# Text shift by transposing sums and one fold, text V shifted while leaving PSUM, one pass per P tile, text gate moved to the output phase: a tuned joint-attention block on one Trainium2 core

## The chip, the cores and the metric

The kernel runs on one core of one Trainium2 chip. The metric is device microseconds from start to end of one execution; lower is better. A run also lists its **span**, which is what the profiler covers of it. For the kernel before, the time is about 1.8 us more than the span.

A ratio below is the mean time of one kernel's runs over the mean of the other's runs of the same rounds, so it is not quite the ratio of the medians quoted beside it.

## The reference

Two streams, image (2 x 256 tokens) and text (2 x 32 tokens), width D = 1152, all bf16. Each is normalised, scaled and shifted by rows computed from `c`, projected to Q, K and V, and attended jointly; the outputs are gated.

```python
mod_i = (_silu(c) @ wmod_img).reshape(B, 6, 1, D)      # shift, scale, gate are the first three
mod_t = (_silu(c) @ wmod_txt).reshape(B, 6, 1, D)
hi = _layernorm(x_img, axis=-1) * (1 + sci) + shi
ht = _layernorm(x_txt, axis=-1) * (1 + sct) + sht
qkvi = hi @ wqkv_img
qkvt = ht @ wqkv_txt
# q, k, v: text tokens and image tokens concatenated, text first
scores = jnp.einsum('bqd,bkd->bqk', q, k) * D ** (-0.5)
p = _softmax(scores, axis=-1)
a = jnp.einsum('bqk,bkd->bqd', p, v)
out_i = x_img + gai * (ai @ wo_img)
out_t = x_txt + gat * (at @ wo_txt)
```

## The kernel before

The order of the work is: normalise the image rows; image V (tiles `vps`) and the image's shift rows; image Q and K (nine blocks each, one 128-column block at a time, tiles `ps`), with the text's small work hung between blocks; text Q and K; scores (`sps`) and softmax; text V; transposes of P (`pT_ps`); attention (`aps`); output products with gate and residual.

Image V is computed without its shift, and the shift's contribution (the row `sv` = shift times the V weights) is added to the attention output instead, because the rows of P sum to one. The text's V must then have the same image row subtracted, so that the addition is right for text keys too. Here, four extra matmuls do that inside the text V products, with a selector `sel` of minus ones:

```python
def v_txt(r):
    ps = ps_mm.tile([P, KT, LW], f32, tag="mm")
    for kt in range(KT):
        for g in range(2):
            mm(ps[64 * g:64 * g + NTT], lhsT=hT_t[:, kt, :], rhs=group(w_v_t, kt, 2 * r + g),
               start=(kt == 0), stop=False, tile_position=(0, 64 * g))
    for g in range(2):
        mm(ps[64 * g:64 * g + NTT], lhsT=sel[:, 2 * r + g, :], rhs=svr[:],
           start=False, stop=True, tile_position=(0, 64 * g))
    return ps

def v_txt_out(r, ps):                      # four VectorE copies, and later one more of the whole tile
    for g in range(2):
        dst = v_t[0:NTT, :].rearrange("p (c g l) -> p g c l", g=NGG, l=LW)[:, 2 * r + g]
        pin(nc.vector.tensor_copy(dst, ps[64 * g:64 * g + NTT]))
```

The text's shift row is `silu(c) @ W`. VectorE multiplies and adds the weights' nine row blocks into `acc_sh` (128 partitions x 1152 for each batch row). The sum over partitions is then made by TensorE: the float32 sums are split into two bf16 halves, and 16 matmuls with a one-column selector `pick` add the partitions:

```python
def vec_split(acc):
    ...
    for b in range(B):
        nc.scalar.copy(hl[:, 0, b, :], acc[:, b, :])
        pin(nc.vector.tensor_sub(hl[:, 1, b, :], acc[:, b, :], hl[:, 0, b, :]))

def vec_rows(hl, gps, strip):
    terms = [(b, t) for b in range(B) for t in range(2)]
    for b, t in terms:
        for g in range(NGG):
            mm(gps[LW * g:LW * g + LW], lhsT=pick[:, b, :], rhs=strip(hl[:, t, b, :], g), ...)
```

P (the softmax result) is written by VectorE in pieces: the 256 image keys, and then the 32 text keys twice, because the attention reads them from two partition ranges. Then P is transposed, copied by ScalarE, and used:

```python
def soft_div(key, parts):
    ...
    pin(nc.vector.tensor_scalar_mul(pb[0:qn, 0:NI], e[0:qn, 0:NI], rs[0:qn, :]))
    for r0, r1, b in parts:
        pin(nc.vector.tensor_scalar_mul(
            pb[r0:r1, NI:PBW].rearrange("p (h b n) -> p b h n", h=2, b=B)[:, b],
            e[r0:r1, NI:NTOK].unsqueeze(1).to_broadcast([r1 - r0, 2, NT]), rs[r0:r1, :]))
```

Each gate row is a product of 36 matmuls; it goes to DRAM and comes back spread over the partitions (`gb` for the image, `gbf` for the text). The DMAs of this trip are issued by POOL:

```python
def mod_rows(w_blk, si):
    ...                                    # 36 matmuls into gps, ScalarE copies them to g_sb
    for b in range(B):
        nc.gpsimd.dma_start(gsc[si, b, :].rearrange("(g j) -> g j", g=NGG), g_sb[b:P:32, :])

def img_gate():
    mod_rows(w_ga_i, 0)
    for b in range(B):
        nc.gpsimd.dma_start(gb[:, b, :], gsc[0, b, :].partition_broadcast(P))
```

The order in this stretch, and the order of the last weight loads on the sync queue:

```python
w_q_t, w_k_t, w_ga_i, w_v_t = ...          # loads, issued early in the program
w_ga_t = load_w(2, wmod_txt, 2 * D)        # text gate weights
w_o_i = load_rows(3, wo_img, 0)            # image output weights, in three parts
w_o_t = load_rows(1, wo_txt, 0)
...
scores and softmax, with img_gate() between   # [cut]
vt = [v_txt(r) for r in range(2)]
v_txt_out(0, vt[0])
p_transposes(0)
p_transposes(1)
v_txt_out(1, vt[1])
pin(nc.vector.tensor_copy(v_t[64:64 + NTT, :], v_t[0:NTT, :]))
txt_gate()
for d0 in range(0, KT, 3):
    attn_pair(...)
out_img(0, C3); out_img(1, C3); out_img(2, C3); out_txt(); out_img(3, ...)
```

## Time and profile before

| | before |
|---|---|
| time, median of the first 3 runs | 118.73 us (118.64 to 118.84) |
| span of the profiled run | 117.0 us, granted clock 0.995 |
| TensorE busy | 111.2 us, 95% |
| VectorE busy | 74.6 us, 64% |
| ScalarE busy | 44.4 us, 38% |
| DMA rate from 12 us to 96 us | about 410 GB/s |

The first section of the page of the kernel before gives busy time, share of the span and count of instructions for each engine; the slices below it give the DMA rate in 40 equal parts of the span.

```profile
...
PE 111.2 (95%) x1046; PEld 63.9 (55%) x1054; DVE 74.6 (64%) x158; ACT 44.4 (38%) x91; POOL 11.1 (10%) x34
...
GB/s 98 368 374 390 409 407 409 411 410 414 411 399 372 410 410 413 404 411 413 413 410 413 414 402 414 414 401 414 408 406 411 406 401 376 177 100 6 101 50 101
...
```

TensorE (PE) is busy nearly all the time, and DMA is full up to slice 33. Busy shares are averages, so they only suggest the bound. The chain of waits shows it: it follows the work that ended last back to its causes, in order of time. Its columns are start, length, and what ran; "issue" is time in which nothing was waited for. These are the pieces of the kernel before that the change touches.

```profile
...
64.32 1.71 PE gps L61 x52
66.02 0.16 issue
...
76.68 2.92 PE sps L61 x36
...
83.02 2.57 PE ps L61 x40
85.59 1.11 PE pT_ps L64 x18
86.70 1.22 PE gps L61 x36
87.92 5.88 PE aps L61 x54
93.81 19.52 PE ps L61 x144
...
113.34 0.44 DVE tmp L690
...
```

From the first of these lines to 113.32 us everything on the chain is TensorE, end to end but for pieces marked "issue" of 0.16 us (66.02) and 0.05 us. The 0.16 us stands where the record of one matmul is missing (17 of 18 are in the trace for the two blocks that follow), so it may be no pause at all. The line of 52 matmuls at 64.32 holds 36 for the text's scale row and the 16 selector matmuls of its shift; the line of 40 at 83.02 holds 36 matmuls of text V and the four selector matmuls; the 36 at 86.70 are the text gate.

What comes off this list comes off the time, as long as no hole opens. VectorE waits on PE in this part, not the other way round. In this trace the text gate weights landed at 85.71 us, 0.9 us before their first use at 86.64, and the last third of the image output weights at 92.98 us, under 2 us before its use.

The cost of the text gate's trip comes from the view of one tile, here `gbf` of the kernel before:

```profile
...
DMA to landing us min/median/max: 3.8/4.8/5.2
```

### The profile page before, as it was taken

The page shows a single profiled execution, that of the slowest core. Times are in us where ns is not written, and L with a number is a line of the kernel's source. Part 1 is how long each engine was busy: PE and PEld are TensorE (multiplying, and loading weights), DVE is VectorE, ACT ScalarE, POOL GpSimd, SP SyncE. Part 2 cuts the span into 40 slices and gives each one's busy share as a digit, 9 for nine tenths or more (in the row PEclk, how much of TensorE's full clock was granted, in tenths as well). Part 3 has the DMA queues.
Part 4 walks back from the last instruction along what each step waited for, and adds up shares of the span by engine and source line. Part 5 has one row for each costly group of instructions (what it writes and reads, how often), then busy time and mean ns, then how long its engine had stood idle before and what let it go on. Part 6 is the DMA issues. An engine that isn't in the chain of part 4 may idle for free.

```text
span 117.0 us, 2513 instructions
## 1 busy us (share of the span) xinstructions
PE 111.2 (95%) x1046; PEld 63.9 (55%) x1054; DVE 74.6 (64%) x158; ACT 44.4 (38%) x91; POOL 11.1 (10%) x34
## 2 busy tenths in 40 slices
PE   4998899999999999999999999999999999999990
PEld 1245544445574444445444658777876666656660
DVE  2368694053867979999996350018984756666671
ACT  4599720042654834325265224245556610000000
POOL 7230000000000000000000000001318018000000
PEclk9999999999999999999999999999999999999998
DMA  3999999999999999999999999999999999520223
GB/s 98 368 374 390 409 407 409 411 410 414 411 399 372 410 410 413 404 411 413 413 410 413 414 402 414 414 401 414 408 406 411 406 401 376 177 100 6 101 50 101
DMA packets 18613, 40.86 MB, mean 349 GB/s; under 512 B 1019, under 2 KB 1547, under 8 KB 18603
## 3 DMA queue, kind: packets, MB, share of 16 engines
q1 hardware_dynamic: 17728, 39.56, 87.0%
q0 software_dynamic: 480, 0.89, 2.1%
q10 hardware_dynamic: 395, 0.26, 0.7%
q8 instruction: 8, 0.13, 0.4%
q14 instruction: 2, 0.02, 0.0%
HBM read 39.38 MB, written 1.34 MB: 348 GB/s over the span
## 4 chain that ended last, share of the span: by engine, by line
PE 85%; ACT 5%; DMA 4%; DVE 2%; issue 1%; DVEq 0%
PE ps L61 53%; PE vps L61 15%; PE gps L61 6%; PE aps L61 5%; PE sps L61 4%; DMA x_i<-in_x_img_dram 4%; ACT xn_i L202 2%; ACT xn_i L201 2%; PE pT_ps L64 1%; DVE xn_i L216 1%; PE tp L64 1%; DVE tmp L690 1%; ACT rstd L211 1%; ACT rstd L212 1%; DVE o L691 0%
## 5 line engine op out<-in xcount | busy, mean ns | idle before, releaser
L61 PE MATMUL ps<-xT_i,t 128*128 128x512 bf16 x157 | 35.2, 380 | 0.4 <-issue 0.2
L61 PEld LDWEIGHTS <-t 128*128 128x128 bf16 x324 | 20.5, 98 | 19.1 <-issue 0.5
L427 DVE SCALAR_TENSOR_TENSOR acc_sh<-t,sTf,acc_sh 128x1152 f32<-128x1152 bf16 x16 | 21.4, 1414 | 0.0
L61 PE MATMUL ps<-t,aT 128*128 128x384 bf16 (+3 forms) x153 | 20.2, 308 | 0.0
L61 PE MATMUL vps<-t,hS_i 128*128 128x512 bf16 (+1 forms) x106 | 17.8, 325 | 0.2
L61 PEld LDWEIGHTS <-aT 128*128 128x128 bf16 (+1 forms) x153 | 13.0, 101 | 7.1 <-issue 0.5
L61 PEld LDWEIGHTS <-hS_i 128*128 128x128 bf16 x108 | 9.0, 98 | 8.8 <-DVE hS_i L268 0.5
L690 DVE TENSOR_TENSOR tmp<-ps,gb 128x384 bf16<-128x384 f32 (+2 forms) x13 | 6.8, 526 | 6.3 <-PE ps L61 6.3
L370 ACT CAST qkT<-ps 128x512 bf16<-128x512 f32 (+2 forms) x11 | 6.0, 552 | 11.0 <-PE ps L61 11.0
L61 PE MATMUL wps<-warm 128*128 128x512 bf16 x24 | 8.1, 498 | 1.7 <-DVE unit L132 1.5
L515 POOL DMA_DIRECT2D mod_scratch<-g_sb x4 | 2.5, 633 | 74.6 <-ACT g_sb L513 74.5
L368 ACT ACTIVATE qkT<-ps 128x512 bf16<-128x512 f32 (+2 forms) x11 | 6.1, 559 | 9.1 <-PE ps L61 9.1
L184 DVE CAST v_i<-vps 128x512 bf16<-128x512 f32 x5 | 3.5, 692 | 7.5 <-PE vps L61 7.5
L554 DVE TENSOR_REDUCE nmx<-sps 128x1 f32<-128x288 f32 x4 | 1.8, 458 | 9.9 <-PE sps L61 9.9
L186 ACT CAST v_i<-vps 128x512 bf16<-128x512 f32 x4 | 2.3, 578 | 10.0 <-PE vps L61 10.0
L623 DVE TENSOR_SCALAR aT<-aps,svc 128x288 bf16<-128x288 f32 x9 | 4.3, 518 | 2.5 <-PE aps L61 2.5
L61 PEld LDWEIGHTS <-warm 128*128 128x128 bf16 x25 | 2.7, 118 | 5.5 <-issue 2.9
L61 PEld LDWEIGHTS <-sT 128*32 128x32 bf16 x180 | 4.6, 96 | 2.0 <-issue 1.3
L61 PE MATMUL sps<-qkT 128*128 128x288 bf16 (+1 forms) x54 | 5.5, 287 | 0.0
L61 PE MATMUL gps<-t,sT 128*32 128x288 bf16 x144 | 5.2, 287 | 0.0
L61 PE MATMUL aps<-pT,v_i 128*128 128x288 bf16 x36 | 5.1, 288 | 0.0
L61 PE MATMUL ps<-hT_t,t 128*128 128x64 bf16 x162 | 5.1, 193 | 0.0
(114 smaller groups left out, 109.2 us busy)
## 6 DMA issues: line engine op xcount, KB each, us to landing
t<-in_wqkv_txt_dram SPq DMA_DIRECT2D x3, 2592.0 KB, 17.8
t<-in_wmod_img_dram SPq DMA_DIRECT2D x2, 2592.0 KB, 13.0
t<-in_wqkv_img_dram SPq DMA_DIRECT2D x2, 2592.0 KB, 20.1
t<-in_wmod_txt_dram SPq DMA_DIRECT2D x2, 2592.0 KB, 15.9
t<-in_wmod_txt_dram SPq DMA_DIRECT2D x3, 864.0 KB, 14.7
t<-in_wo_img_dram SPq DMA_DIRECT2D x3, 864.0 KB, 12.8
t<-in_wo_txt_dram SPq DMA_DIRECT2D x3, 864.0 KB, 12.6
t<-in_wqkv_img_dram SPq DMA_DIRECT2D x3, 576.0 KB, 9.1
```

The source lines that it names most:

```text
L61: return pin(nc.tensor.matmul(*a, **k))
L64: return pin(nc.tensor.transpose(*a, **k))
L184: nc.vector.tensor_copy(out_ap, in_ap)
L186: nc.scalar.copy(out_ap, in_ap)
L201: pin(nc.scalar.activation(junk, x_ap, ACT.Copy, scale=1.0 / D, accum_out=sm[:, 0:1]))
L202: pin(nc.scalar.activation(junk, x_ap, ACT.Square, scale=float(D) ** -0.5, accum_out=sm[:, 1:2]))
L368: nc.scalar.mul(out_ap, in_ap, SCALE)
L370: nc.scalar.copy(out_ap, in_ap)
L427: pin(eng.scalar_tensor_tensor(acc[:, b, :], w[:, kt, :], sTf[:, kt, b:b + 1], acc[:, b, :], op0=ALU.mult, op1=ALU.add))
L515: nc.gpsimd.dma_start(gsc[si, b, :].rearrange("(g j) -> g j", g=NGG), g_sb[b:P:32, :])
L623: nc.vector.tensor_scalar(dst, tiles[(b, dt)][:], bias, None, op0=ALU.add)
L690: nc.vector.tensor_mul(tmp[:, 0:n], ps[:, 0:n], gb[:, b, c0:c0 + n])
```

## The change

The intent is to take 20 selector matmuls out of TensorE's stream, and to arrange the rest so that TensorE still waits for nothing.

1. **Text shift.** VectorE sums the accumulated products in blocks of 32 with a transposing reduce, which leaves 36 columns in place of 1152 for each batch row, 72 in all; two matmuls with a folding matrix and two small VectorE instructions finish it.
2. **Text V.** The image row `sv` is written to DRAM and spread over the text rows by DMA (`svb`), and VectorE subtracts it while the product leaves PSUM. The loads from the text's K weights on are issued after this spread.
3. **P tiles.** VectorE writes 288 columns in one pass; POOL writes the second copy of the 32 text columns. The transposes of P come right after the scores, and the second group's PSUM copy is split over two tiles. The loads of the image gate are issued by POOL behind these writes (`img_gate_spread`).
4. **Text gate.** Its matmuls and its DRAM trip move from before the attention to the middle of the output products. The image output weights are therefore loaded before the text gate's weights.
5. The text's normalisation moves from VectorE to ScalarE, and some loads are cut differently.

```diff
+    w_o_i = load_rows(4, wo_img, 0)                 # now first ...
+    w_ga_t = load_w(3, wmod_txt, 2 * D)             # ... and the text gate's weights after it
...
+        for b in range(B):
+            nc.scalar.dma_start(svd[b].rearrange("(c g l) -> g c l", g=NGG, l=LW), svr[b:P:LW])
+        for g in range(2):
+            for b in range(B):
+                r0 = 64 * g + NT * b
+                nc.sync.dma_start(svb[r0:r0 + NT, :], svd[b, g * HD:(g + 1) * HD].partition_broadcast(NT))
...
-    def vec_split(acc): ...
-    def vec_rows(hl, gps, strip): ...
+    def shift_blocks():
+        for b in range(B):
+            pin(nc.vector.tensor_reduce(uf[:, b, :], acc_sh[:, b, :].rearrange("p (c l) -> p c l", l=LW),
+                                        axis=AX.X, op=ALU.add, apply_transpose=True))
+        pin(nc.vector.tensor_copy(ub[:, 0], uf[:]))
+        pin(nc.vector.tensor_sub(ub[:, 1], uf[:], ub[:, 0]))
+    def shift_fold():
+        ps = ps_tr.tile([P, B * KT, NGG], f32, tag="tr", name="shps")
+        for h in range(2):
+            mm(ps[:].rearrange("p k a -> p (k a)"), lhsT=fold[:].rearrange("p g l -> p (g l)"),
+               rhs=ub[:, h].rearrange("p b c -> p (b c)"), start=(h == 0), stop=(h == 1))
+        ...                                          # mask with band, sum 4 columns each
...
-        for g in range(2):
-            mm(ps[64 * g:64 * g + NTT], lhsT=sel[:, 2 * r + g, :], rhs=svr[:], ...)
...
+        pin(nc.vector.tensor_sub(v_t[:, r * VC:(r + 1) * VC], ps[:], svb[:, r * VC:(r + 1) * VC]))
...
-        pin(nc.vector.tensor_scalar_mul(pb[0:qn, 0:NI], e[0:qn, 0:NI], rs[0:qn, :]))
-        for r0, r1, b in parts: ...
+        pin(nc.vector.tensor_scalar_mul(pb[0:qn, 0:NTOK], e[0:qn, :], rs[0:qn, :]))
+        pin(nc.gpsimd.tensor_scalar(pb[0:qn, NI + 2 * NT:NI + 3 * NT], e[0:qn, NI:NTOK], rs[0:qn, :], 0.0,
+                                     op0=ALU.mult, op1=ALU.add))
...
-    vt = [v_txt(r) for r in range(2)]
-    v_txt_out(0, vt[0])
     p_transposes(0)
+    for r in range(2):
+        v_txt_out(r, v_txt(r))
     p_transposes(1)
-    txt_gate()
+    img_gate_spread()
...
-    out_img(1, C3)
+    out_img(1, C3, between=txt_gate)
```

## The prediction

> **What bounds it now.** TensorE. The profile page's first section has PE busy 95% of a 117.0 us span at a granted clock of 0.995. In the chain of waits PE is 85%; from 12.5 us to 113.3 us it is nearly unbroken matmul. PE's list of waits holds 1.5 us before warm-up and 0.6 us of crumbs. VectorE (64%) and ScalarE (38%) bind nowhere in between. DMA is full (about 410 GB/s) until 97 us, but PE never waits for a weight. Only what leaves PE's stream, or opens a hole in it, can move the time.
>
> **What leaves PE** (chain of waits, in order of time):
> - Sixteen selector matmuls of the text shift. 52 matmuls took 1.71 us at 64.3 us; the same 36 alone took 1.22 us elsewhere: 0.49 us. Two folding matmuls of 72 columns replace them, estimated 0.1 us.
> - Four matmuls that subtract the image's shift row from text V: 40 matmuls took 2.57 us, 36 by their spacing 2.31 us: 0.26 us.
> - The 36 text gate matmuls (1.22 us) move to the output phase; not saved.
>
> Sum: about -0.65 us, all on the chain.
>
> **Off the chain.** VectorE loses two subtractions of 1.36 us, the text normalisation (0.86), eight small P writes (0.24 each), four V evictions (0.45) and a copy (0.45); it gains two transposing sums (estimated 1.3 us each) and small ones. ScalarE: -2.3 us of copies, +1.3 us of normalising. POOL: five writes of 32 columns.
>
> **Where a hole could open.**
> 1. Fold, at block 7 of K. VectorE's sums done by 63 us, fold near 67 us; the text activations then need about 1.3 us while PE has 1.97 us of block 7. No wait.
> 2. First P transposes now follow the scores directly (near 82.5 us). The text P tile is written about then; POOL's part comes behind its two DMA issues. Wait 0 to 0.3 us. v_txt then covers the second group's softmax and the PSUM copies.
> 3. Attention starts about 1.8 us earlier (near 86.0), outputs near 92. Image gate rows landed near 95 before; VectorE will wait for them at the first output chunk, but six PSUM buffers absorb it.
> 4. The text gate makes its DRAM round trip during output: store issued near 100 us, landing near 103.7, loads to about 109, against text output's first PSUM at 107.6. This trace shows 3.8 to 5.2 us to landing per hop. The Trainium skill ("DMA: Bandwidth & Descriptors", Anatomy of one DMA) gives about 2.0 us fixed; the trace's numbers are used. VectorE may stand 1.5 us, then recovers 0.5 us per chunk before the last; most of it vanishes.
>
> **Prediction: 118.1 us**, range 117.4 to 118.9. Chance of over 2% faster 0.04, within 2% 0.92, over 2% slower 0.04.
>
> **What would show it right.** Outputs start about 1.8 us earlier, and the gain shrinks to 0.6 us once the gate matmuls run there; PE's idle time unchanged; selector groups gone; VectorE's busy time down some 6 us without effect on the end; a VectorE wait at the first gate product and perhaps at the text output.
>
> **What would make it wrong.** Text gate landing after 111 us: VectorE ends last, slower by 1 us or more. PE waiting on POOL at the P transposes or on VectorE before text Q. Smaller DMAs on the sync queue delaying weights. A larger gain would need idle time in the head to shrink; its chain (input DMA, ScalarE sums, normalisation) is untouched.

## The result, and the profile after

| | before | after |
|---|---|---|
| median of 6 runs | 118.78 us (118.54 to 118.88) | 118.15 us (118.08 to 118.50) |
| ratio | | 0.9954, 95% interval 0.9938 to 0.9969 |
| span of the profiled run | 117.0 us, clock 0.995 | 116.3 us, clock 1.0 |

The time is 118.15 us where 118.1 was predicted. The verdict at 2% is "same"; the gain of half a per cent is outside the noise of these runs. A second series, on another chip, did not show it by time (after_again below).

The first section of the page of the kernel after:

```profile
...
PE 110.3 (95%) x1036; PEld 63.3 (54%) x1036; DVE 71.9 (62%) x151; ACT 44.8 (38%) x93; POOL 12.3 (11%) x34
...
```

TensorE's busy time is 0.9 us lower, VectorE's 2.7 us. The chain of waits of the kernel after, over the same stretch:

```profile
...
60.26 1.22 PE gps L61 x36
...
67.41 0.07 PE shps L61 x2
...
76.29 2.93 PE sps L61 x36
...
82.63 0.50 PE pT_ps L64 x9
83.13 2.33 PE ps L61 x36
85.46 0.61 PE pT_ps L64 x9
86.07 5.78 PE aps L61 x54
91.84 5.85 PE ps L61 x36
97.69 1.22 PE gps L61 x36
98.91 13.77 PE ps L61 x108
...
112.71 0.43 DVE tmp L693
...
```

The scale row is 36 matmuls alone (1.22 us), the shift two matmuls in 0.07 us, and text V 36 matmuls in 2.33 us. The text gate (1.22 us at 97.69) now stands between two pieces of the output products. TensorE is again unbroken.

The two chains can be cut at the same points and compared. Each number is the difference of two starts in the chains above and their earlier lines (first image V matmul at 14.53 us before and 14.37 after).

| stage | before, us | after, us | difference |
|---|---|---|---|
| start to first image V matmul | 14.53 | 14.37 | -0.16 |
| first image V matmul to scores | 62.15 | 61.92 | -0.23 |
| scores to attention | 11.24 | 9.78 | -1.46 |
| attention | 5.89 | 5.77 | -0.12 |
| outputs, to VectorE's last four instructions | 19.53 | 20.87 | +1.34 |
| VectorE's last four instructions | 1.22 | 1.21 | -0.01 |

The -1.46 is the gate's 1.22 leaving and 0.24 of text V; the +1.34 is the gate's 1.22 coming back and 0.12 more. The sum from the first image V matmul on is -0.48 us. I use this stretch, **from the first image V matmul to the end of VectorE's last output instruction**, as the yardstick for single profiles below: 100.03 us before, 99.55 us after. It leaves out the head, whose end depends on when the image scale weights land, and which none of the five parts was meant to touch. The clock is no rival to it: the windows view gives a granted clock of 1.00 from 15 us to 113 us in all kernels but onepass_only; the 0.995 of the kernel before comes from the time after its last matmul.

Two of VectorE's groups after (line, engine, operation, output<-input, count | busy us, mean ns | idle before, releaser) show the transposing sums and one large idle time:

```profile
...
L445 DVE TRANSPOSE_TENSOR_REDUCE uf<-acc_sh 128x36 f32<-128x1152 f32 x2 | 2.6, 1346 | 0.0
...
L455 DVE TENSOR_TENSOR uf<-shps,band 128x72 f32<-128x72 f32 x1 | 0.2, 233 | 4.4 <-PE shps L61 4.4
...
```

The transposing sums took 1.35 us each, as estimated. The 4.4 us in front of `uf<-shps` is VectorE waiting for TensorE to reach the fold, so the fold had that much slack.

Two more numbers were different from what was predicted. The text gate's trip back, by the view of the tile `gbf` of the kernel after:

```profile
...
DMA to landing us min/median/max: 2.0/2.2/2.5
```

And the DMA rate while the spread of the V shift was under way, by the view of windows (busy time and count of each engine, clock, DMA share, GB/s), first of the kernel before and then of the kernel after:

```profile
...
58.00:62.00 4.00, 4.00 (x21) 1.76 (x19) 4.00 (x4) 2.54 (x3) 0.00 (x0) 1.00 1.05 414
...
```

```profile
...
58.00:62.00 4.00, 4.00 (x50) 2.00 (x49) 3.86 (x6) 1.17 (x2) 0.00 (x0) 1.00 1.06 353
...
```

The DMA engines were as busy as before but moved 353 GB/s in place of 414. What this costs is the subject of several experiments.

### The profile page after: what moved, and what is told of

It is laid out like the page before. It is cut to its first block, busy times and chain, and to the rows that moved or that the text cites. A ratio compares the mean times of both kernels' runs of the same rounds, so it can differ in the third digit from the quotient of the medians.

```text
span 116.3 us, 2500 instructions
## 1 busy us (share of the span) xinstructions
PE 110.3 (95%) x1036; PEld 63.3 (54%) x1036; DVE 71.9 (62%) x151; ACT 44.8 (38%) x93; POOL 12.3 (11%) x34
## 3 DMA queue, kind: packets, MB, share of 16 engines
HBM read 39.52 MB, written 1.34 MB: 351 GB/s over the span
## 4 chain that ended last, share of the span: by engine, by line
PE 86%; DMA 8%; DVE 1%; SPq 1%; issue 0%; DVEq 0%
PE ps L61 53%; PE vps L61 15%; DMA t<-in_wmod_img_dram 8%; PE gps L61 5%; PE aps L61 5%; PE sps L61 5%; PE pT_ps L64 1%; PE sc_ps L61 1%; SPq L104 1%; PE tp L64 1%; DVE tmp L693 1%; DVE o L694 0%; SPq L108 0%; PE tpt L64 0%; DVE hS_i L264 0%
## 5 line engine op out<-in xcount | busy, mean ns | idle before, releaser
L61 PE MATMUL ps<-xT_i,t 128*128 128x512 bf16 x162 | 35.7, 379 | 0.0
L580 POOL TENSOR_SCALAR pb<-e,rs 128x32 bf16<-128x32 f32 (+1 forms) x5 | 2.1, 415 | 74.7 <-DVE rs L577 74.6
L61 PE MATMUL wps<-warm 128*128 128x512 bf16 x25 | 7.4, 452 | 1.5 <-DVE unit L127 1.5
```

Of the source, the lines that this page charges most:

```text
L61: return pin(nc.tensor.matmul(*a, **k))
L580: pin(nc.gpsimd.tensor_scalar(pb[0:qn, NI + 2 * NT:NI + 3 * NT], e[0:qn, NI:NTOK], rs[0:qn, :], 0.0, op0=ALU.mult, op1=ALU.add))
```

## The experiments

**Theory A**: the gain is what left TensorE's stream, 0.49 us for the fold and 0.26 us for text V less about 0.1 for the folding matmuls; everything else is neutral. **Rival B**: VectorE's lighter load is what gains (softmax, P tiles and evictions come sooner, and TensorE meets fewer late inputs). After the first four runs a third one was formed, called **E**: the V spread by DMA costs about one microsecond by delaying all later weights, and the new order of weights with the late text gate is what makes that free. The remaining parts are then not gains of their own but conditions for the others.

For reference, the yardstick of every profile, and the mean of what each kernel's timed runs took beyond their spans. Ratios are against the kernel before on the same chip.

| kernel | median, us | ratio, 95% interval | yardstick, us | time less span, us |
|---|---|---|---|---|
| before (three chips) | 118.60 to 118.81 | | 100.03 | 1.79 to 1.82 |
| after | 118.15 | 0.9954 (0.9938 to 0.9969) | 99.55 | 2.03 |
| fold_only | 118.35 | 0.9968 (0.9947 to 0.9990) | 99.60 | 1.80 |
| vshift_only | 119.83 | 1.0085 (1.0060 to 1.0110) | 100.71 | 2.04 |
| onepass_only | 124.50 | 1.0488 (1.0462 to 1.0514) | 105.59 | 1.79 |
| gate_late_only | 119.51 | 1.0080 (1.0048 to 1.0112) | 100.65 | 1.83 |
| gate_back | 120.47 | 1.0166 (1.0143 to 1.0189) | 101.13 | 2.09 |
| pe_back | 118.99 | 1.0028 (1.0008 to 1.0049) | 100.09 | 2.05 |
| dve_back | 118.35 | 0.9980 (0.9951 to 1.0009) | 99.44 | 2.06 |
| spread_only | 119.73 | 1.0088 (1.0067 to 1.0108) | 100.64 | 2.03 |
| after_again | 119.04 | 1.0008 (0.9961 to 1.0055) | 99.58 | 2.10 |
| dve_back_again | 118.70 | 0.9997 (0.9958 to 1.0036) | 99.41 | 2.09 |
| onepass_pinned | 118.58 | 0.9998 (0.9958 to 1.0037) | 100.01 | 1.82 |
| gate_later | 119.46 | 1.0066 (1.0025 to 1.0108) | 100.37 | 1.96 |

The first four kernels do one part alone on the kernel before. All kernels gave correct results.

### fold_only: the text shift's sums and fold alone

```diff
-    def vec_split(acc): ...          # and vec_rows, txt_rows_shift, txt_cols_shift
+    def shift_blocks(): ...          # as after
+    def shift_fold(): ...
-    qk_img(w_k_i, 1, {1: (txt_transposes, txt_shift_split,),
-                      6: (txt_rows_scale, txt_rows_shift, txt_cols_shift, txt_modulate),
+    qk_img(w_k_i, 1, {1: (txt_transposes, shift_blocks,),
+                      6: (txt_rows_scale, shift_fold, txt_modulate),
```

> The kernel before with the folded text shift alone: transposing sums and one pair of 72-column matmuls in place of the sixteen selector matmuls, everything else as before. Theory A (what leaves TensorE's stream is the gain): 0.49 us leave, about 0.07 to 0.1 us come, so -0.40 us, ratio to before about 0.9966, and the chain's TensorE piece at the folded place 0.4 us shorter. Rival B (relief of VectorE and ScalarE is the gain): VectorE loses only 2.7 us of subtractions and gains 2.6 us of sums here, so about 0. Rival C (a shorter head or a better order of DMAs is the gain): 0.

Measured: 118.35 us against 118.71, ratio 0.9968; the yardstick is 0.43 us shorter. The chain of waits of this kernel:

```profile
...
64.29 1.22 PE gps L61 x36
...
65.67 10.55 PE ps L61 x189
...
```

Scale row and fold now take 1.38 us from 64.29 to 65.67, where the kernel before took 1.86 (64.32 to 66.18, with the 0.16 us at the missing record in it). The safer number is the stretch from the first image V matmul to the first score matmul in the traces: 61.56 us against 61.99, or 0.43 us less. Theory A holds for this part, and the fold is the only part that gains by itself.

### vshift_only: the V shift at the eviction alone

```diff
-            mm(ps[64 * g:64 * g + NTT], lhsT=sel[:, 2 * r + g, :], rhs=svr[:], ...)
+            nc.sync.dma_start(svb[r0:r0 + NT, :], svd[b, g * HD:(g + 1) * HD].partition_broadcast(NT))
+        pin(nc.vector.tensor_sub(v_t[:, r * VC:(r + 1) * VC], ps[:], svb[:, r * VC:(r + 1) * VC]))
     # the loads from w_k_t on follow the spread on the sync queue, as after; their own order is before's
```

> The kernel before with text V's shift taken off while leaving PSUM (rows spread by DMA, four matmuls gone), the V text tile in two halves, and the six last weight loads issued after the shift rows in program order. Theory A: four matmuls, two at a time, are 0.24 to 0.26 us of TensorE's stream, so -0.25 us, ratio about 0.998. Rival B: VectorE loses 1.2 us between scores and attention, but TensorE waits for none of it, so under A nothing further; if relief there matters it would show as more than -0.4 us. Rival C: 0.

Measured: 119.83 us, ratio 1.0085. This was a miss: a gain was expected and there is a loss of a microsecond. TensorE's waits in this kernel (longest first: engine, tile, line, what it waited for, us in total, times, longest):

```profile
...
PE gps L61 <- DMA t<-in_wmod_txt_dram: 0.6, 1, 0.6
```

Its chain of waits goes through a weight load for the first time:

```profile
...
79.91 15.25 DMA t<-in_wo_img_dram
...
95.21 18.70 PE ps L61 x138
...
```

The text gate's weights landed at 86.91 us (85.71 before), the last third of the image output weights at 95.17 (92.98 before). The yardstick closes, by the starts of TensorE's instructions: from the first text V matmul to the gate +0.41 (-0.24 for the four matmuls, +0.65 at the gate's weights, of which the list of waits shows 0.59), and +0.26 in the outputs, where the seventh matmul starts at 95.21 us, 0.43 us after the sixth in place of 0.16; together with under 0.02 elsewhere that is the measured +0.68. So DMA was a second bound just under the first. My reading "PE never waits for a weight" was true and misleading.

### spread_only: the DMA spread alone, with nobody using it

This was run later, to separate the spread from the eviction.

```diff
     # kernel before, selector matmuls and all
+        for b in range(B):
+            nc.scalar.dma_start(svd[b].rearrange("(c g l) -> g c l", g=NGG, l=LW), svr[b:P:LW])
+        for g in range(2):
+            for b in range(B):
+                nc.sync.dma_start(svb[r0:r0 + NT, :], svd[b, g * HD:(g + 1) * HD].partition_broadcast(NT))
     # the loads from w_k_t on follow it on the sync queue
```

> The kernel before plus the spread of the shift rows by DMA into a tile that nobody reads, with the six last weight loads issued after it in program order; all matmuls and VectorE work as before. Theory E (DMA was the second bound, with under 1 us to spare at the text gate and under 2 us at the output weights): later weights land 1.0 to 1.2 us later, TensorE waits for the text gate weights or for the last rows of the image output weights, +1.0 to +1.5 us, ratio 1.008 to 1.013. If the loss of the run with the V shift alone came from its new V tile, row order or VectorE work instead: 0, ratio 1.000.

Measured: 119.73 us, ratio 1.0088, the same loss as vshift_only within the noise (yardstick 100.64 against 100.71). Its chain of waits holds the same weight load, 15.25 us long and ending at 95.44. The window of the spread:

```profile
...
58.00:62.00 4.00, 4.00 (x19) 1.79 (x19) 4.00 (x4) 1.75 (x3) 0.00 (x0) 1.00 1.06 352
...
```

So the spread alone makes the loss of vshift_only; the four matmuls that leave there gain nothing, because the last weights land no sooner. The four DMAs carry 147 KB, and the window lost 62 GB/s for 4 us, or 248 KB. Together, at 411 GB/s, that is an estimate of 0.96 us of DMA time. The landings agree: text Q's weights landed at 61.07 us against 59.78 and text K's at 67.79 against 66.22, but the text's scale weights, ahead of the spread, were already 0.60 us later in this profile (53.98 against 53.38). From the scale weights to text K's it took 13.81 us against 12.84, or 0.97 us more (vshift_only 13.85, the kernel after 13.82). The packets in the traces show where it went: those of the spread took 0.44 us of the 16 engines' time, and the weights' packets of 2,304 bytes took 108 to 111 ns each from 58 to 62 us in place of 93. The Trainium skill, in "DMA: Bandwidth & Descriptors", section "Issuing engines are not separate DMA queues", says that DMAs started by different engines run on the same 16 DMA engines and interleave. The interleaving shows here: text Q's weights were issued at 38.5 us, before the spread, and landed late all the same. Both were issued by the sync engine, though, so this run doesn't test engines against each other; the traces of the text gate do (POOL's loads, 3.8 to 5.2 us with the sync engine's weights under way and 2.0 to 2.5 us without), and they are in line with the page.

### onepass_only: the P tiles in one VectorE pass and POOL's copy alone

```diff
-        pin(nc.vector.tensor_scalar_mul(pb[0:qn, 0:NI], e[0:qn, 0:NI], rs[0:qn, :]))
-        for r0, r1, b in parts: ...
+        pin(nc.vector.tensor_scalar_mul(pb[0:qn, 0:NTOK], e[0:qn, :], rs[0:qn, :]))
+        pin(nc.gpsimd.tensor_scalar(pb[0:qn, NI + 2 * NT:NI + 3 * NT], e[0:qn, NI:NTOK], rs[0:qn, :], 0.0,
+                                     op0=ALU.mult, op1=ALU.add))
```

> The kernel before with one VectorE pass per P tile and the repeated 32 columns written by POOL, nothing else. Theory A: no matmul leaves, and before's TensorE did not wait for the P tiles, so 0 within 0.1 us (ratio 0.999 to 1.001). Rival B: VectorE is lighter by some 1.2 us just before the P transposes, so a gain of some 0.2 us or more.

Measured: 124.50 us, ratio 1.0488, a loss of 5.8 us. This was the largest miss. TensorE's waits:

```profile
...
PE pT_ps L64 <- POOL pb L569: 2.8, 1, 2.8
...
PE pT_ps L64 <- DVE pb L568: 0.9, 1, 0.9
```

The order of POOL's instructions in this kernel (start, length, instruction, idle time before it and its releaser):

```profile
...
81.61 1.51 POOL L515 DMA_DIRECT2D mod_scratch<-g_sb  x2 [0.70 <-ACT g_sb L513]
87.57 1.13 POOL L524 DMA_DIRECT2D gb<-mod_scratch  x2 [4.46 <-DMA mod_scratch<-g_sb]
88.74 0.56 POOL L569 TENSOR_SCALAR pb<-e,rs 64x32 bf16<-64x32 f32 x2
...
```

POOL issues the image gate's store, then stands 4.46 us until that store has landed because its next instruction is the issue of the load, and only then writes text P. The short P writes take 0.3 to 0.5 us; the wait in front of them is what costs. TensorE's two waits are 3.7 us of the 5.56 us that the yardstick lost. The rest is in the chain right behind them:

```profile
...
90.32 0.93 PE pT_ps L64 x7
91.25 2.28 PE gps L61 x28
93.53 5.99 PE aps L61 x54
...
```

The text gate's 36 matmuls (the chain counts 28 of them) took 2.35 us here by the view of the timeline, against 1.29 us in the kernel before. From 90.3 us to 93.7 us the granted clock was 0.50. Half of these 3.4 us, an estimate of 1.7 us, closes the sum to within 0.2 us. All five timed runs of this kernel show a mean clock of 0.969 to 0.986. The lower clock came right after the pause and is absent in onepass_pinned, where the pause is gone; what sets it was not tested.

The Trainium skill, in "PSUM — Partial Sum Buffer", section "Engine vs sequencer instructions", says that the queues of ScalarE, VectorE and GpSimdE are strict FIFO; this timeline agrees, and shows that the issue of a DMA that must wait holds the computing instructions behind it as well.

### onepass_pinned: the same, with the gate's load behind POOL's writes

This was run later, to confirm the reading.

```diff
     # onepass_only
-            nc.gpsimd.dma_start(gb[:, b, :], gsc[0, b, :].partition_broadcast(P))      # in img_gate()
+            pin(nc.gpsimd.dma_start(gb[:, b, :], gsc[0, b, :].partition_broadcast(P))) # after the P transposes' code
```

> The kernel before with one VectorE pass per P tile and POOL's repeat, and the image gate's loads pinned behind POOL's writes, as the whole change has them. If the 5.8 us loss of the run without the pin came from POOL's queue alone (a write to P standing behind a DMA that waits for its landing), this is 0 within 0.2 us of before, ratio 0.998 to 1.002, and TensorE shows no wait for POOL. If the pass itself or the other column offset costs, a loss of 0.3 us or more stays.

Measured: 118.58 us, ratio 0.9998, yardstick 100.01 against 100.03. POOL's order is now this:

```profile
...
81.45 1.51 POOL L515 DMA_DIRECT2D mod_scratch<-g_sb  x2 [0.70 <-ACT g_sb L513]
82.99 0.30 POOL L571 TENSOR_SCALAR pb<-e,rs 64x32 bf16<-64x32 f32 x1
...
87.42 1.17 POOL L526 DMA_DIRECT2D gb<-mod_scratch  x2 [2.48 <-DMA mod_scratch<-g_sb]
...
```

Text P is written 1.5 us after the store's issue in place of 7, and the loss is gone. The one-pass write by itself is worth nothing, because it unloads VectorE where VectorE has time. That the diff moves this load behind the P writes is not tidying: on the kernel before, the one pass without it lost 5.8 us. The whole change without it was not run. VectorE did 1.0 us less work here (73.5 us busy against 74.6), just before the P transposes, and the yardstick didn't move: that speaks against rival B at this place.

### gate_late_only: the text gate in the output phase alone

```diff
-    txt_gate()
-    out_img(1, C3)
+    out_img(1, C3, between=txt_gate)
     # and the residual's text rows are loaded with the image gate, as after
```

> The kernel before with the 36 text gate matmuls moved into the output phase, after the fourth output chunk, and the order of V and P transposes left as before. Theory A with covers: the matmuls are only moved, but before's order used their 1.2 us to cover ScalarE's two copies of the transposed P (0.88 us each) and VectorE's copies of text V. Without them attention waits, so +0.3 to +0.6 us, and TensorE's waits show the copies. Rival D (the gate's new place is itself a gain): -0.2 us or better. Plain count of matmuls without covers: 0.

Measured: 119.51 us, ratio 1.0080; the direction was right and the loss larger (0.62 us by the yardstick, 0.5 us of it a wait). The chain of waits:

```profile
...
85.69 0.62 PE pT_ps L64 x9
...
86.34 0.89 ACT pT L611
...
87.27 5.94 PE aps L61 x54
...
```

With the gate's matmuls gone from before the attention, TensorE reaches the attention while ScalarE is still copying the transposed P (0.89 us at 86.34), and TensorE waits 0.5 us. In the kernel before, the gate was cover for that copy. In the kernel after, other work is: the P transposes of the first group come before text V (2.33 us), so their copy is done in its shadow, and the second group's copy is split. That order needs P early, which is why the one-pass write belongs to the change; this last link is read from the order of the code and was not tested by itself.

### gate_back: the kernel after with the text gate back before the attention

```diff
-    w_o_i = load_rows(4, wo_img, 0)
-    w_ga_t = load_w(3, wmod_txt, 2 * D)
+    w_ga_t = load_w(2, wmod_txt, 2 * D)
+    w_o_i = load_rows(4, wo_img, 0)
+    txt_gate()                                  # before the attention
-    out_img(1, C3, between=txt_gate)
+    out_img(1, C3)
```

> The kernel after with the text gate put back in front of attention and its weights loaded ahead of the image output weights again (the load order of before); the V spread by DMA stays. If the gate's new place is worth nothing by itself (the prediction's view: only moved), the time stays at that of after, ratio to before 0.9954. If the new place is what pays for the spread's DMA time (theory E, from the run with the V shift alone, where every later weight landed 1.0 to 1.2 us late), the text gate weights land near 87 us, TensorE needs them near 86.1, waits about 0.8 us, and the image output weights' last rows come just in time or late: +0.8 to +1.3 us on after, ratio to before 1.002 to 1.006.

Measured: 120.47 us, ratio 1.0166, more than expected. TensorE's waits:

```profile
...
PE gps L61 <- DMA t<-in_wmod_txt_dram: 1.4, 1, 1.4
...
```

The gate's weights landed at 86.96 us, and TensorE was ready for them 1.44 us earlier: later weights and an earlier consumer. The yardstick is 1.58 us above the kernel after, 101.13 against 99.55. So the late gate together with the output weights ahead of it in the queue is what pays for the spread; the two were only undone together. In the kernel after, the gate's weights landed only at 95.78 us, and they were needed at 97.69.

### pe_back: the kernel after with TensorE's removed work put back

```diff
-        rows["sc"] = mod_rows_of(w_sc_t, sT32)
+        rows["sc"] = mod_rows_of(w_sc_t, sT32, extra=4)        # 16 more matmuls, results overwritten
+        for g in range(2):                                     # in v_txt: 2 more matmuls for each half
+            mm(ps[64 * g:64 * g + NTT, :], lhsT=hT_t[:, 0, :], rhs=w_v_t[:, 0, g * HD:g * HD + VC],
+               start=True, stop=True, tile_position=(0, 64 * g))
```

> The kernel after with as many idle matmuls as the change took away: sixteen 32-column-tile matmuls of 288 columns ahead of the text scale rows and four 64-column-tile ones in front of text V, into the same PSUM before the real start, so the result stays right. Theory A (the gain is TensorE's stream): the 0.49 + 0.25 us come back, so after + 0.7 us, ratio to before 1.000 to 1.002. Rival B (VectorE's and ScalarE's relief is the gain): stays at that of after, 0.9954.

Measured: 118.99 us, ratio 1.0028, yardstick 100.09. The chain of waits shows the two groups at their old lengths:

```profile
...
60.43 1.71 PE gps L61 x52
...
83.59 2.57 PE ps L61 x40
...
```

VectorE keeps its lighter load here, and the whole gain is gone. This speaks for theory A and against B. Everything else of the change is kept too, the text's normalisation on ScalarE and the new cuts and order of the loads (part 5 and rival C, neither run by itself): together with the two folding matmuls it nets 0.06 us on the yardstick (100.09 against 100.03), so no gain is left for it to explain.

### dve_back and dve_back_again: the kernel after with VectorE work put back

```diff
         pin(nc.vector.tensor_sub(ub[:, 1], uf[:], ub[:, 0]))
+        for n in range(3):                                     # 4.1 us of VectorE, nobody reads it
+            dead = work.tile([P, D], bf, tag="dead", bufs=1, name="dead")
+            pin(nc.vector.tensor_sub(dead[:], acc_sh[:, n % B, :], x_i[:, n, :]))
```

> The kernel after with three dead VectorE subtractions of 1152 elements (about 1.36 us each, 4.1 us) right behind the two sums, in front of the text scale. VectorE then has put back more than the change took from it there. Theory A: VectorE waited 4.4 us for the fold in after, so the sums still end before TensorE comes to the fold; no change against after, ratio to before 0.9954 within 0.001. Rival B: a good part of the gain is lost, ratio 0.998 or more.

Measured in the first run: 118.35 us, ratio 0.9980 with an interval from 0.9951 to 1.0009. That interval holds both theories' numbers, so the times decided nothing. The trace did: the 4.14 us were done at 65.7 us, VectorE still waited 0.55 us for the fold's matmuls, and the yardstick was 99.44 us. VectorE's timeline:

```profile
...
61.52 4.14 DVE L451 TENSOR_TENSOR dead<-acc_sh,x_i 128x1152 bf16<-128x1152 f32 x3
...
67.66 0.23 DVE L458 TENSOR_TENSOR uf<-shps,band 128x72 f32<-128x72 f32 x1 [0.55 <-PE shps L61]
...
```

The same kernel was run again beside the kernel after on one chip, with this expectation:

> The kernel after with the three dead VectorE subtractions, run once more beside the control, because the first time its interval held both answers. Theory A: the same time as the control within 0.15 us, span 116.1 to 116.4 us. Rival B: 0.25 us or more above the control, span 116.5 us or more.

Measured: 118.70 us, below its control at 119.04, yardstick 99.41 against 99.58. Putting back more VectorE time than the change took away (4.1 us against 2.7 net) cost nothing that the yardstick shows, and nothing by time within the noise. Rival B is refuted, at this place in the program.

### after_again: the control on another chip

The kernel is unchanged.

> The kernel after, unchanged, as the control on the same chip as the others of this call. Ratio to before 0.9954 within 0.0015; the span near 116.1 to 116.3 us.

Measured: 119.04 us, ratio 1.0008 with an interval from 0.9961 to 1.0055, so the gain of the first runs was not seen again by time. This is a miss. The chain of waits of its profile shows where the time was:

```profile
...
2.12 10.50 DMA t<-in_wmod_img_dram
...
15.11 13.77 PE vps L61 x63
...
```

The scale weights landed at 12.62 us where they landed at 11.85 in the first profile, and the first image V matmul began 0.74 us later. From there on it took 99.58 us against 99.55. So the yardstick of the kernel after is reproduced to 0.03 us (that of the kernel before has one profile, and onepass_pinned, with the same matmuls, has 100.01), but a head that varies by more than the gain can hide it. On this chip the kernel before varied from 118.01 to 119.46 us.

### gate_later: the text gate one output block later still

```diff
-    out_img(1, C3, between=txt_gate)
-    out_img(2, C3)
+    out_img(1, C3)
+    out_img(2, C3, between=txt_gate)
```

> The kernel after with the text gate three output chunks (4.4 us) later. By the prediction's own reasoning on the gate's two DRAM hops, with the 2.0 to 3.4 us per hop that after's trace shows in this phase: store near 104 us, loads landing near 111 us, VectorE stands from 107.6 to 111 us, does 1.5 us for the text and 3.1 us for four image chunks, and ends near 115.6 us instead of 113.9: +1.3 to +2.0 us on after, ratio to before 1.006 to 1.012. If only the count of matmuls mattered: 0.9954.

Measured: 119.46 us, ratio 1.0066; the yardstick is 100.37, or 0.82 us above the kernel after. The mechanism is as expected and the size smaller. The chain of waits ends in VectorE:

```profile
...
101.83 1.25 PE gps L61 x36
...
103.78 1.66 DMA mod_scratch<-g_sb
...
107.36 3.02 DMA gbf<-mod_scratch
...
111.67 0.56 DVE tmp L693
...
```

The store landed 1.66 us after its issue and the last load 3.02 us after its own, at 110.38 us where the expectation had about 111; VectorE then works almost without a pause from 110.5 us to the end, for 4.1 us where 4.6 were expected. The kernel after escapes this: its loads had landed by 106.98 us, 0.6 us before the text's first product at 107.6.

## Why the prediction was right, and where it was wrong

**The bound and the sum: right.** TensorE's stream bounds both kernels. Taken alone, the fold was worth 0.43 us on the yardstick (0.39 by the prediction's sum of 0.49 less 0.1), and text V 0.24 us in the stage from scores to attention (0.26 predicted). pe_back takes the gain away, dve_back and dve_back_again do not.

**The gate moved and was not saved: right.** It left the stage before the attention (1.22 us) and came back in the outputs, with 0.12 us on top. Outputs began 1.97 us earlier (91.84 against 93.81), of which the head is 0.16; the prediction said about 1.8.

**No wait at the fold and at the P transposes: right.** VectorE's sums were done at 61.0 us and its scaling of the text at 63.1 us; it then waited 4.4 us for the fold. TensorE's list of waits has no entry for either place.

**Waits of VectorE: wrong.** The prediction said "VectorE will wait for them at the first output chunk" and "may stand 1.5 us" at the text output. It waited for TensorE only. The image gate's rows had landed, the first at 92.46 us, and the first product began at 93.34 us. The failing term was "landed near 95 before": in the kernel before the first landed at 94.39 us after a trip of 6.9 to 7.6 us, and after the change the trip took 5.4 to 6.1 us. Why it was shorter was not separated. At the text output the failing term was the trip: "3.8 to 5.2 us to landing per hop" had been read while the last weights were still arriving (the last one landed at 101.49 us in the kernel before). After the change the last weights landed at 102.11 us. The store, issued at 99.65 us, still met them and took 3.0 to 3.4 us; the loads, issued from 103.31 us on, took 2.0 to 2.5 us. The Trainium skill's figure of about 2.0 us fixed per DMA ("DMA: Bandwidth & Descriptors", Anatomy of one DMA), which the prediction set aside, fits the loads after the weights were in; the trace's number fits the full queues. The same page, in the section "Latency and other measured facts", says that HBM access latency is 0.2 us on average and 2 us at high load, and that a lighter load makes the fixed cost smaller. The direction agrees with these two traces. So neither number was wrong; I took a duration from a stage with a different load.

**VectorE's busy time: wrong size, no effect.** "VectorE's busy time down some 6 us" came to 2.7 us. The prediction's own items give 7.75 us that leave and 2.6 us of sums that come, which is 5.15 and not 6, before its "small ones". It counted eight small P writes where the kernel before has six. The small ones that it left without a number came to some 2.7 us: the fold's four instructions (0.9), the subtractions at the eviction (1.1), building `fold` and `band` (0.6) and wider P writes (0.1); small copies of 0.65 us that left were not counted either. dve_back_again shows that 4.1 us more, put at the fold, did not matter.

**"PE never waits for a weight": right for both kernels, but it was taken for slack.** The slack was 0.9 us at the gate's weights, and the spread costs about 1.0 us. In vshift_only and spread_only the weights become the bound. The prediction listed "smaller DMAs on the sync queue delaying weights" as a risk; the delay did come, and the new order of loads paid for it. The result was right although this step was not worked out.

**What the sum left out.** Three small terms partly cancel. The head was 0.16 us shorter in the first profile by chance; after_again shows that it can be 0.58 us longer than before's 14.53. The stretch to the scores was 61.92 and 61.95 us in the two profiles of the kernel after, against 61.73 to 61.81 in fold_only, dve_back_again and gate_later, so 0.1 to 0.2 us were lost there in those two runs. The traces show the place: between the 38th and 39th matmul of text K, starts are 0.22 and 0.25 us apart in these two, 0.07 and 0.10 in dve_back_again and gate_later, and 0.03 elsewhere in the group. And every kernel with the V spread takes 1.96 to 2.10 us beyond its span on average, every kernel without it 1.79 to 1.83: about 0.2 us of the gain is lost where the profile does not look. That the total met the prediction within 0.05 us is therefore partly luck; the parts on TensorE's stream are not.

**Open.** Why the spread's loads slow the weights' packets beside them was not separated: their rows are 1,152 bytes, and each is read 32 times. The stores of 64 bytes are not the reason: in spread_only they moved from 39.5 to 41.8 us, and the rate was 411 GB/s from 40 to 44 us, against 412 before. Where the 0.2 us beyond the span come from is not known, and neither is what causes the pause in text K. gate_back's timed spans (mean 118.4 us) were longer than the profiled one (117.6), so its loss of 1.58 us by the yardstick is a lower figure than the timed one.

None of these runs pointed to a version that would beat the kernel after, and none was tried.

## What to carry to other kernels

When one engine's stream is unbroken, add up only what leaves it, and for each other resource look up the slack, not whether it was waited for: a DMA queue that is never waited for can still be 0.9 us from being the bound. Parts of a change can be conditions for one another, so a part that gains nothing or loses alone (here three of four) may still be needed; undo it in the full version before judging it. Take the duration of a DMA trip from a stage with the same load on the queues, and never put a computing instruction behind a DMA issue that has to wait on the same in-order queue.

## What the Trainium skill lacked or had wrong

- "DMA: Bandwidth & Descriptors" gives about 2.0 us fixed per DMA. That fits the loads in the kernel after once the weights were in (2.0 to 2.5 us for 36 KB; 2.6 to 3.3 us in gate_later), but the page has no figure for a small trip while the queues are full: 3.8 to 5.2 us for the same transfer while the last weights were arriving, and 6.9 to 7.6 us for the image gate's 288 KB in the kernel before.
- The same page names 512 bytes as the smallest transfer for line rate. While four DMAs with rows of 1,152 bytes, each read 32 times, were under way, the rate was 352 to 356 GB/s in place of 412 to 414, with the DMA engines as busy as before; the weights' own packets took 107 to 111 ns in place of 93. No run separates the row size from the repeated reading.
- "PSUM — Partial Sum Buffer" has the strict order of GpSimdE's queue, but no page says what follows for a kernel that mixes computing and DMA issues there: one load that had to wait for its store held a 0.3 us write back and cost 5.8 us (onepass_only), some 3.7 us of it as waits and the rest in the slower clock behind them.
- No page has the time of a transposing sum on VectorE: 1.35 us for 128 x 1152 float32.
- No page says what can lengthen an execution outside the profiled span: 1.96 to 2.10 us there in kernels with the V spread through DRAM against 1.79 to 1.83 without, and 2.03 against 1.82 in spread_only, which adds the spread and issues six loads after it.
